# One block of state increments per unit, state products beside the chunk products, and a new table of steps

## The chip, the cores and the metric

One core of one Trainium2 chip runs the whole kernel. The metric is the device time of one execution in microseconds. Engines are named as the profile names them: PE is TensorE, ACT is ScalarE, DVE is VectorE, POOL is GpSimd, SP is SyncE; PE, ACT, DVE and POOL each run their own stream of instructions in program order, and SP mainly issues DMAs. PSUM is the memory into which TensorE writes its products.

## The reference, cut to what matters

```python
f = 1.0 / (1.0 + np.exp(-f_logit))
for t in range(S):                        # B, H, S, D = 4, 8, 768, 48
    state = f[:, :, t, :, None] * state + k_t v_t^T      # per batch and head, D x D
    y[:, :, t] = q_t @ state
x = y transposed to (B*S, H*D)            # 3072 x 384
h = x @ w_in                              # 384 x 2048
P = a0 + a1*h + a2*h**2 + a3*h**3
Q = 1 + |b0|*|h| + |b1|*h**2
out = (P / (Q + 1e-6)) @ w_out            # 2048 x 384
```

A gated linear recurrence over 768 time steps, then a feed-forward block whose activation is a rational function.

## The kernel before

**Units.** The time axis is cut into chunks of 128 steps, and two chunks of one batch element make a unit n = 4c + b (b the batch element, c = 0, 1, 2 the place in time). There are twelve units of 256 time steps. Each runs through the recurrence and then through the feed-forward block; the state of a batch element is handed from unit n to unit n + 4.

**The recurrence of a unit, by steps.** `ld` loads f, k, q and v. `ef` and `ls` (ACT) make the logarithms of the gates, `cs` (PE) sums them within a chunk, `A` (ACT, x = 0 or 1) takes the exponentials of the sums with either sign, `xa` (DVE) multiplies q and k by them, `T` (PE) and `Te` (DVE) transpose both. `sc` (PE) makes the scores within a chunk in two groups, `mk` (DVE) masks them, `vm` (POOL, or ACT in unit 0) copies pieces of v. `ya n j` (PE) does four things for chunk j: the products of q with the state at the beginning of the chunk (line 387, twelve products 128x32, left out where the state is zero), the increments k v of the chunk (line 410, sixteen products of 64 rows by 64 columns), the old state added to them through the identity (line 413), and, for j = 0, the decays summed over each chunk (line 417). `ae` (ACT) takes the exponential of the decays, `st n j` (DVE, line 446) multiplies and writes the state, in place: a batch element has one state buffer. So `ya n 1` waits for `st n 0`, and `st n j` may overwrite the state only after the products that read it. In the last third of the units (c = 2) chunk 1 needs no new state. `yb` (PE) adds the 64 products of the masked scores with v to the same y (64x32 each), and `ye` (ACT) writes y to SBUF as x.

**The feed-forward block.** `h` (PE) makes four of the sixteen blocks of 128 hidden units, in twelve products; `hy` (ACT) copies them. h squared comes from `sq` (DVE) or `sa` (ACT), |h| from `ab` (DVE). The denominator h^2 + |h| is summed either by `u` (PE, identity products into PSUM) and read by `ln` (ACT), or by `zd` (an adding DMA that POOL issues) or `zv` (DVE) and read by `lz` (ACT). `ex` (ACT) takes exp(-ln). `p1`, `p2`, `pm` (DVE), `ta` (an adding DMA) or `tv` (DVE), and `gm` (DVE) make the numerator and the quotient; `o` (PE) multiplies by w_out, `oe` copies, `so`, `s0`, `s1` store.

**What sets the order.** Everything. `ORDER` is a table of steps written out by hand or by a planner; the loop at the end of the kernel calls them one by one, and each engine gets its instructions in that order. Numbers after a step's name are the unit and blocks, `@i` is one of four PSUM slots of two banks each. A slot is given to the next step that names it once its last reader is done. `ya n 0 @i @j` takes a slot for y, which it holds until `ye`, and one for the state sums.

**The start.** `hv` writes two elements of w_in ahead of the load `wi 0 4`, so that this load waits for DVE to get there. a and b are loaded from ACT's queue (`ab_`), `fa` and `fb` (DVE) make the scaled coefficients, `rg` (ACT) loads two of them as registers, which `ye` and `ln` use. v of unit 0 comes as float32 into a buffer of its own, v32, and `vc` (ACT) casts it.

Of the kernel before, what the change touches and what calls it, by code (L numbers as in the profile page):

```python
# [19 lines left out]
ab_; cz 2; cb; ld 0 f 2 4; ld 0 f 0 2; ca; cz 3; ld 0 q 2 4; cz 1; ld 0 k 2 4; cz 0; cc; ld 0 k 0 2  # L20
ef 0 2 4; ls 0 2 4; ld 0 q 0 2; ef 0 0 2; fa; cs 0 2 4 @0; ls 0 0 2; ld 0 v; A 0 0 2 4; cs 0 0 2 @1
fb; A 0 1 2 4; xa 0 0 2 4; ld 1 f; rg; xa 0 1 2 4; A 0 0 0 2; T 0 2 4 @0; A 0 1 0 2; ld 1 k
Te 0 2 4; xa 0 1 0 2; sc 0 1 @0; ld 1 q; hv 0; xa 0 0 0 2; wi 4 8; mk 0 1; T 0 0 2 @1; vc 0
Te 0 0 2; vm 0 1 s; ya 0 0 @0 @2; vm 0 0 s; wi 0 4; sc 0 0 @1; ae 0; ef 1; ld 2 f; st 0 0; mk 0 0
ya 0 1; ls 1; ld 1 v; yb 0 2 4; st 0 1; yb 0 0 2; wi 8 16; cs 1 @1; ye 0; A 1 0; h 0 4 8 @0; A 1 1
hy 0 4 8; xa 1 1; ld 2 k; h 0 0 4 @0; xa 1 0; ld 2 q; hy 0 0 4; T 1 @1; ab 0 0 8; sq 0 0 8; ef 2
ld 3 f; Te 1; u 0 0 4 @0; ls 2; vm 1 1; ya 1 0 @2 @3; p1 0 0 8; vm 1 0; ln 0 0 4; ld 2 v; cs 2 @1
p2 0 0 8; ae 1; sc 1 0 @0; st 1 0; A 2 1; ld 3 k; mk 1 0; ya 1 1; A 2 0; xa 2 1; sc 1 1 @1
u 0 4 8 @0; st 1 1; mk 1 1; ln 0 4 8; ld 3 q; pm 0 0 8; ex 0 0 8; yb 1; h 0 12 16 @1; wo 8 12
xa 2 0; ye 1; wo 0 4; tv 0 0 8; ld 4 f; h 0 8 12 @0; ef 3; wo 4 8; gm 0 0 8; hy 0 12 16; wo 12 16  # L30
h 1 4 8 @2; hy 0 8 12; h 1 12 16 @1; ls 3; ld 4 k; sq 0 8 16; sa 1 4 8; vm 2 1; h 1 8 12 @0
p1 0 8 16; hy 1 12 16; ld 3 v; ab 0 8 16; hy 1 4 8; h 1 0 4 @3; vm 2 0; pm 0 8 16; hy 1 8 12
p2 0 8 16; u 0 12 16 @2; sa 1 0 4; ld 4 q; sq 1 8 16; u 0 8 12 @0; ln 0 12 16; T 2 @1; tv 0 8 16
ln 0 8 12; cs 3 @2; Te 2; hy 1 0 4; o 0 0 0 4 @0; o 0 1 0 4; A 3 1; ab 1 8 16; sc 2 0 @3; ab 1 0 8
A 3 0; u 1 12 16 @1; mk 2 0; ex 0 8 16; u 1 4 8 @2; ld 5 f; p1 1 0 16; u 1 0 4 @3; ln 1 4 8
o 0 1 4 8; gm 0 8 16; ln 1 12 16; o 0 0 4 8; p2 1 0 16; sc 2 1 @2; ln 1 0 4; o 0 1 8 12; u 1 8 12 @1
ef 4; mk 2 1; o 0 1 12 16; ex 1 0 8; pm 1 0 8; ya 2 0 @2 @3; ld 5 k; o 0 0 8 12; xa 3 1; ta 1 0 8
ae 2; ln 1 8 12; o 0 0 12 16; st 2 0; ls 4; xa 3 0; ya 2 1; ex 1 8 16; ld 5 q; pm 1 8 16; yb 2
T 3 @1; ld 4 v; st 2 1; ye 2; cs 4 @3; Te 3; ta 1 8 16; oe 0 0 2 s; h 2 12 16 @2; vm 3 1; A 4 1
ld 6 f; vm 3 0; A 4 0; sc 3 1 @1; xa 4 1; h 2 8 12 @0; hy 2 12 16; xa 4 0; so 0 0 2; ef 5  # L40
h 2 4 8 @3; mk 3 1; hy 2 8 12; sc 3 0 @2; gm 1 0 8; hy 2 4 8; h 2 0 4 @1; sa 2 4 8; mk 3 0; ld 6 k
o 1 0 0 4 @0; hy 2 0 4; o 1 0 4 8; sq 2 8 16; ld 5 v; sa 2 0 4; ya 3 0 @2 @3; ab 2 0 8; vm 4 1
o 1 1 0 4; ae 3; ab 2 8 16; ls 5; vm 4 0; o 1 1 4 8; zd 2 0 8; st 3 0; u 2 8 12 @1; p1 2 0 16
# [12 lines left out]
ya 5 1; mk 5 1; lz 4 0 8; so 2 0 2; cs 7 @0; zv 4 8 16; yb 5; u 3 8 12 @1; A 7 1; ld 8 v; st 5 1
ye 5; p1 4 0 16; T 6 @3; vm 7 0; ln 3 8 12; vm 7 1; h 5 4 8 @2; gm 3 0 8; A 7 0; ld 8 q; ex 3 8 16
h 5 12 16 @0; Te 6; p2 4 0 16; o 3 0 0 4 @3; ex 4 0 8; sc 6 1 @1; o 3 0 4 8; gm 3 8 16; o 3 1 0 4
ld 9 f; hy 5 12 16; xa 7 1; o 3 1 4 8; o 3 0 8 12; hy 5 4 8; mk 6 1; h 5 0 4 @0; sa 5 4 8; pm 4 0 8
ld 9 k; ef 8; h 5 8 12 @1; xa 7 0; ta 4 0 8; hy 5 0 4; o 3 0 12 16; pm 4 8 16; hy 5 8 12; sc 6 0 @2  # L60
o 3 1 8 12; sa 5 0 4; mk 6 0; ta 4 8 16; o 3 1 12 16; lz 4 8 16; ya 6 0 @0 @1; p1 5 0 16; ld 9 q
T 7 @2; ab 5 8 16; ae 6; oe 3 0 2 s; st 6 0; ex 4 8 16; sq 5 8 16; ya 6 1; so 3 0 2; yb 6; ab 5 0 8
u 5 8 12 @3; st 6 1; vm 8 0; ye 6; Te 7; zd 5 0 8; u 5 12 16 @1; ef 9; vm 8 1; ln 5 8 12; h 6 0 4 @0
pm 5 8 16; ld 9 v; ln 5 12 16; p2 5 0 16; h 6 12 16 @3; hy 6 0 4; ld 10 f; gm 4 0 8; ta 5 8 16
sc 7 0 @1; sa 6 0 4; h 6 8 12 @2; hy 6 12 16; mk 7 0; sc 7 1 @0; ls 8; o 4 0 0 4 @3; gm 4 8 16
hy 6 8 12; h 6 4 8 @1; mk 7 1; ld 10 k; ex 5 8 16; o 4 0 4 8; sq 6 8 16; ya 7 0 @0 @2; hy 6 4 8
pm 5 0 8; o 4 0 8 12; ae 7; sa 6 4 8; o 4 1 0 4; p1 6 0 16; ta 5 0 8; o 4 1 4 8; lz 5 0 8; ld 10 q
o 4 1 8 12; st 7 0; cs 8 @1; pm 6 0 8; ls 9; ya 7 1; pm 6 8 16; ex 5 0 8; yb 7; o 4 0 12 16; st 7 1
vm 9 0; ab 6 0 8; o 4 1 12 16; vm 9 1; ye 7; ld 10 v; ab 6 8 16; cs 9 @2; oe 4 0 2 s; gm 5 8 16
h 7 12 16 @0; zd 6 0 8; A 8 1; so 4 0 2; p2 6 0 16; A 8 0; h 7 4 8 @3; hy 7 12 16; xa 8 1; ta 6 8 16  # L70
h 7 8 12 @1; ef 10; xa 8 0; ta 6 0 8; ld 11 f; hy 7 4 8; h 7 0 4 @0; gm 5 0 8; hy 7 8 12; zv 6 8 16
T 8 @3; A 9 1; hy 7 0 4; o 5 0 0 4 @1; xa 9 1; o 5 1 0 4; lz 6 8 16; Te 8; o 5 0 4 8; ld 11 k
o 5 0 8 12; sq 7 0 8; A 9 0; sc 8 1 @3; sc 8 0 @0; ex 6 8 16; o 5 0 12 16; mk 8 1; o 5 1 4 8; xa 9 0
o 5 1 8 12; lz 6 0 8; ya 8 0 @3 @2; mk 8 0; ld 11 q; o 5 1 12 16; sq 7 8 16; ae 8; ex 6 0 8; T 9 @0
st 8 0; ab 7 8 16; ya 8 1; yb 8; ab 7 0 8; oe 5 0 2 s; u 7 8 12 @2; Te 9; vm 10 0; ye 8; zd 7 0 8
u 7 12 16 @1; ls 10; gm 6 8 16; vm 10 1; so 5 0 2; h 8 12 16 @0; ln 7 8 12; ld 11 v; gm 6 0 8
ln 7 12 16; sc 9 1 @2; cs 10 @3; p1 7 0 16; hy 8 12 16; h 8 8 12 @1; A 10 0; mk 9 1; ex 7 8 16
o 6 0 0 4 @0; p2 7 0 16; o 6 1 0 4; sc 9 0 @2; o 6 1 4 8; A 10 1; pm 7 0 8; o 6 1 8 12; hy 8 8 12
o 6 1 12 16; mk 9 0; ta 7 0 8; ef 11; ya 9 0 @1 @3; lz 7 0 8; pm 7 8 16; h 8 4 8 @2; xa 10 1
# [35 lines left out]
def kernel(  # L115
# [16 lines left out]
    P = 128  # L132
# [479 lines left out]
```

## Time and profile before

| | |
|---|---|
| median of three runs | 236.91 us (236.08 to 237.78) |
| span of the profiled execution | 231.9 us |
| granted TensorE clock, mean | 0.992 |
| `op` products with w_out (line 556) | 384, 69.7 us busy |
| `hp` products with w_in (line 455) | 576, 67.7 us |
| `u` identity products (line 489) | 88, 13.5 and 13.2 us |
| state increments `sv` (line 410) | 320, 9.2 us |
| state products of y (line 387, `qkT,state`) | 240, 7.2 us |
| `lq<-z` on ACT (line 513) | 13, mean 1952 ns |
| `lq<-u` on ACT (line 497) | 22, mean 1059 ns |
| `state` on DVE (line 446) | 20, mean 550 ns |
| adding DMAs `gall<-hy`, `z<-h` | 21 and 10, 512 KB each, 6.9 and 6.7 us from issue to landing |

A row of the profile's groups names the line, the engine, the operation and the tiles (out<-in), then the count, the busy time and the mean of one. Neighbouring instructions of one engine overlap a little in the records, so a sum of means is larger than an engine's busy time. The ends of matmuls are modelled. The slices cut the span into 40 equal parts, each digit a busy share in tenths. The chain of waits follows the work that ended last back to the start.

### The profile page before, as it was taken

Reading aid. Unit: us, or ns where it says so; the run is one execution under the profiler, and the core shown is the slowest. Engines: PE = TensorE matmul, PEld = TensorE weight load, DVE = VectorE, ACT = ScalarE, POOL = GpSimd, SP = SyncE. Lnnn points to the kernel's source line nnn. Section 1 sums busy time; section 2 is a strip of 40 time slices with the busy share of each in tenths; the row PEclk is TensorE's granted clock in tenths of the full one; section 3 lists DMA queues with packets and bytes.
Section 4 is the critical chain, followed back from the end, with each engine's and each line's share of the span. In section 5 each row is a group of like instructions: output and inputs, shape, how many; then the busy total and the mean of one; then the engine's idle time right before and its main releaser. Section 6 shows DMA issues by size and latency. Waiting matters only on the chain.

```text
span 231.9 us, 7110 instructions
## 1 busy us (share of the span) xinstructions
PE 211.8 (91%) x3120; PEld 146.2 (63%) x3120; DVE 205.4 (89%) x243; ACT 203.3 (88%) x216; POOL 67.7 (29%) x92
## 2 busy tenths in 40 slices
PE   0778679999999999999999999979999999999991
PEld 0455338745876768657767669556677687676550
DVE  6743778999899799999999999979999999899960
ACT  4455559999996999999999999889999999999970
POOL 7261620002405406135118058003231211340100
PEclk9999889999999999999999999999999999999999
DMA  6999999992999999999999968998970994999614
GB/s 146 229 232 204 235 203 203 244 248 72 158 237 251 145 174 231 144 173 183 246 203 215 236 126 154 210 211 164 133 148 16 181 200 82 187 197 204 123 52 119
DMA packets 61694, 41.28 MB, mean 178 GB/s; under 512 B 51424, under 2 KB 57312, under 8 KB 61664
## 3 DMA queue, kind: packets, MB, share of 16 engines
q0 software_dynamic: 19360, 21.57, 57.4%
q1 hardware_dynamic: 41856, 19.08, 35.7%
q8 instruction: 24, 0.39, 0.6%
q10 hardware_dynamic: 448, 0.20, 0.3%
q14 instruction: 6, 0.05, 0.1%
HBM read 25.17 MB, written 4.72 MB: 129 GB/s over the span
## 4 chain that ended last, share of the span: by engine, by line
PE 55%; DVE 21%; DMA 9%; ACT 9%; issue 4%; POOL 1%; POOLq 0%
PE op L556 18%; PE hp L455 15%; PE u L489 7%; DMA z<-h 4%; PE y L387 4%; DVE gall L536 4%; DMA v<-in_v_dram 3%; DVE scm L370 3%; ACT hy L469 3%; PE cs L316 2%; PE sv L410 2%; PE tp L341 2%; DVE gall L549 2%; DVE h L473 2%; DVE z L481 2%
## 5 line engine op out<-in xcount | busy, mean ns | idle before, releaser
L556 PE MATMUL op<-w_out_sb,gall 128*128 128x384 bf16 x384 | 69.7, 326 | 0.7 <-DVE osb L571 0.6
L455 PE MATMUL hp<-xT,w_in_sb 128*128 128x256 bf16 x576 | 67.7, 274 | 1.1 <-ACT hy L469 1.1
L455 PEld LDWEIGHTS <-w_in_sb 128*128 128x128 bf16 x576 | 55.9, 98 | 10.4 <-issue 1.6
L556 PEld LDWEIGHTS <-gall 128*128 128x128 bf16 x384 | 35.9, 98 | 23.8 <-issue 1.2
L469 ACT CAST hy<-hp 128x1024 bf16<-128x1024 f32 x48 | 48.8, 1040 | 2.1 <-PE hp L455 2.1
L521 ACT ACTIVATE qi<-lq 128x2048 bf16<-128x2048 f32 (+1 forms) x25 | 46.8, 1885 | 0.1
L540 POOL DMA_DIRECT2D gall<-hy x21 | 19.3, 969 | 66.7 <-ACT alast L442 24.4
L370 DVE TENSOR_TENSOR scm<-sc,mask 128x1024 bf16<-128x1024 f32 x24 | 29.0, 1216 | 2.6 <-PE sc L362 2.4
L549 DVE TENSOR_TENSOR gall<-gall,qi 128x2048 bf16<-128x2048 bf16 (+1 forms) x25 | 29.3, 1176 | 0.4 <-ACT qi L521 0.3
L536 DVE TENSOR_TENSOR gall<-gall,h 128x2048 bf16<-128x2048 bf16 (+1 forms) x25 | 29.2, 1174 | 0.0
L513 ACT ACTIVATE lq<-z 128x2048 f32<-128x2048 bf16 x13 | 25.4, 1952 | 1.8 <-DMA z<-h 1.8
L497 ACT ACTIVATE lq<-u 128x1024 f32<-128x1024 f32 x22 | 22.3, 1059 | 5.0 <-PE u L489 5.0
L381 POOL COPY vmp<-vn 128x128 bf16<-128x128 bf16 x22 | 16.4, 780 | 34.4 <-PE y L387 14.0
L325 ACT ACTIVATE A<-cs 128x768 f32<-128x768 f32 (+1 forms) x26 | 19.5, 788 | 1.7 <-PE cs L316 1.6
L506 POOL DMA_DIRECT2D z<-h x10 | 9.6, 956 | 37.0 <-ACT h L477 12.9
L473 DVE TENSOR_TENSOR h<-hy 128x2048 bf16<-128x2048 bf16 (+1 forms) x17 | 19.6, 1152 | 0.7 <-ACT hy L469 0.7
L481 DVE TENSOR_SCALAR z<-hy 128x2048 uint16<-128x2048 uint16 (+1 forms) x25 | 16.3, 669 | 2.6 <-ACT hy L469 2.6
L477 ACT ACTIVATE h<-hp 128x1024 bf16<-128x1024 f32 x16 | 17.1, 1070 | 0.0
L526 DVE TENSOR_SCALAR gall<-hy,a_sb 128x4096 bf16<-128x4096 bf16 (+2 forms) x15 | 17.1, 1138 | 0.0
L531 DVE TENSOR_SCALAR hy<-hy,a_sb 128x4096 bf16<-128x4096 bf16 (+2 forms) x15 | 16.9, 1125 | 0.1
L316 PE MATMUL cs<-lsp,Ui 128*128 128x384 bf16 (+1 forms) x39 | 11.6, 358 | 5.8 <-ACT lsp L306 5.8
L330 DVE TENSOR_TENSOR qkp<-kn,A 128x768 bf16<-128x768 f32 (+1 forms) x13 | 11.8, 909 | 4.5 <-ACT A L325 4.4
(70 smaller groups left out, 284.9 us busy)
## 6 DMA issues: line engine op xcount, KB each, us to landing
gall<-hy POOLq DMA_DIRECT2D x21, 512.0 KB, 6.9
z<-h POOLq DMA_DIRECT2D x10, 512.0 KB, 6.7
fn<-in_f_logit_dram SPq DMA_DIRECT2D x11, 384.0 KB, 7.8
kn<-in_k_dram SPq DMA_DIRECT2D x11, 384.0 KB, 9.2
qn<-in_q_dram SPq DMA_DIRECT2D x11, 384.0 KB, 8.2
out_dram<-osb SPq DMA_DIRECT2D x22, 192.0 KB, 4.0
vn<-in_v_dram POOLq DMA_DIRECT2D x11, 192.0 KB, 8.3
w_out_sb<-in_moe_w_out_dram POOLq DMA_DIRECT2D x4, 384.0 KB, 11.4
```

What stands on the lines that cost most here:

```text
L325: nc.scalar.activation(t, src, AF.Exp, scale=1.0 if x else -1.0)
L370: nc.vector.tensor_mul(t, s["sc", g].rearrange("s r a i t -> s (r a) (i t)"), mb)
L455: nc.tensor.matmul(t[:, m - m0, :].rearrange("f (j t) -> f j t", j=UB), w_in_sb[:, kk, m * P:(m + 1) * P], s["x"][:, :, kk, :], start=(kk ...
L469: nc.scalar.copy(fl(big(s, "hy", "hy", 3), m0, m1), fl(s["hp", m0], 0, m1 - m0))
L473: nc.vector.tensor_mul(fl(big(s, "h2", "h2", 2), m0, m1), fl(s["hy"], m0, m1), fl(s["hy"], m0, m1))
L481: nc.vector.tensor_scalar(fl(big(s, "z", "z", 2), m0, m1).bitcast(U16), fl(s["hy"], m0, m1).bitcast(U16), 0x7FFF, None, op0=ALU.bitwise_and)
L497: nc.scalar.activation(fl(s["lq", g], m0 - 8 * g, m1 - 8 * g), fl(s["u", m0], 0, m1 - m0), AF.Ln, scale=rsig2, bias=1.0 + 1e-6)
L513: nc.scalar.activation(fl(s["lq", g], m0 - 8 * g, m1 - 8 * g), fl(s["z"], m0, m1), AF.Ln, scale=rsig2, bias=1.0 + 1e-6)
L521: nc.scalar.activation(fl(s["qi", g], m0 - 8 * g, m1 - 8 * g), fl(s["lq", g], m0 - 8 * g, m1 - 8 * g), AF.Exp, scale=-1.0)
L536: nc.vector.tensor_mul(fl(s["g"], m0, m1), fl(s["g"], m0, m1), fl(s["h2"], m0, m1))
L549: nc.vector.tensor_mul(fl(s["g"], m0, m1), fl(s["g"], m0, m1), fl(s["qi", g], m0 - 8 * g, m1 - 8 * g))
L556: nc.tensor.matmul(s["op"][:, j, 0:DM], s["g"][:, m, C * j:C * j + C], w_out_sb[:, m, :], start=(m == 0), stop=(m == KF - 1))
```

## The change

The state of a batch element gets three buffers that are used in turn, so `st n j` writes a new one instead of the one it read. That frees the products of y with the state from their place: they move from `ya` to the head of `yb`, next to the chunk products, and y takes its slot only there. `ya` is split into `sv`, which makes the increments of both chunks in one run, the chunks (that is, the two row halves) alternating, and `id n j`, which adds the old state and, for j = 0, the decays. The three buffers need room, which v32 gives up: it uses one of the output buffers. a and b are loaded from SP's queue. The table of steps is new from end to end; the `u`, `ln`, `lz`, `zv`, `sa` and `sq` steps in it differ in number. Its purpose is that the state chain no longer holds up the y products, that TensorE changes its shape of product less often, and that slots are held for less time.

```diff
 ORDER = """
...
-ab_; cz 2; cb; ld 0 f 2 4; ld 0 f 0 2; ca; cz 3; ld 0 q 2 4; cz 1; ld 0 k 2 4; cz 0; cc; ld 0 k 0 2
-ef 0 2 4; ls 0 2 4; ld 0 q 0 2; ef 0 0 2; fa; cs 0 2 4 @0; ls 0 0 2; ld 0 v; A 0 0 2 4; cs 0 0 2 @1
-fb; A 0 1 2 4; xa 0 0 2 4; ld 1 f; rg; xa 0 1 2 4; A 0 0 0 2; T 0 2 4 @0; A 0 1 0 2; ld 1 k
-Te 0 2 4; xa 0 1 0 2; sc 0 1 @0; ld 1 q; hv 0; xa 0 0 0 2; wi 4 8; mk 0 1; T 0 0 2 @1; vc 0
-Te 0 0 2; vm 0 1 s; ya 0 0 @0 @2; vm 0 0 s; wi 0 4; sc 0 0 @1; ae 0; ef 1; ld 2 f; st 0 0; mk 0 0
-ya 0 1; ls 1; ld 1 v; yb 0 2 4; st 0 1; yb 0 0 2; wi 8 16; cs 1 @1; ye 0; A 1 0; h 0 4 8 @0; A 1 1
-hy 0 4 8; xa 1 1; ld 2 k; h 0 0 4 @0; xa 1 0; ld 2 q; hy 0 0 4; T 1 @1; ab 0 0 8; sq 0 0 8; ef 2
-ld 3 f; Te 1; u 0 0 4 @0; ls 2; vm 1 1; ya 1 0 @2 @3; p1 0 0 8; vm 1 0; ln 0 0 4; ld 2 v; cs 2 @1
-p2 0 0 8; ae 1; sc 1 0 @0; st 1 0; A 2 1; ld 3 k; mk 1 0; ya 1 1; A 2 0; xa 2 1; sc 1 1 @1
-u 0 4 8 @0; st 1 1; mk 1 1; ln 0 4 8; ld 3 q; pm 0 0 8; ex 0 0 8; yb 1; h 0 12 16 @1; wo 8 12
-xa 2 0; ye 1; wo 0 4; tv 0 0 8; ld 4 f; h 0 8 12 @0; ef 3; wo 4 8; gm 0 0 8; hy 0 12 16; wo 12 16
-h 1 4 8 @2; hy 0 8 12; h 1 12 16 @1; ls 3; ld 4 k; sq 0 8 16; sa 1 4 8; vm 2 1; h 1 8 12 @0
...
+cz 2; ca; ld 0 f 2 4; ld 0 f 0 2; cz 1; ld 0 q 2 4; cz 0; cb; cz 3; ld 0 k 2 4; cc; ef 0 2 4
+ld 0 k 0 2; ls 0 2 4; ld 0 q 0 2; ef 0 0 2; cs 0 2 4 @0; ls 0 0 2; ld 0 v; A 0 1 2 4; cs 0 0 2 @1
+A 0 0 2 4; ab_; xa 0 0 2 4; A 0 0 0 2; A 0 1 0 2; xa 0 1 2 4; ld 1 f; hv 0; T 0 2 4 @1; wi 0 4
+xa 0 1 0 2; xa 0 0 0 2; Te 0 2 4; ld 1 k; T 0 0 2 @0; ld 1 q; wi 4 8; sc 0 1 @1; Te 0 0 2; vc 0
+mk 0 1; sc 0 0 @0; vm 0 0 s; sv 0 @2; vm 0 1 s; mk 0 0; ld 1 v; id 0 0; fa; wi 8 16; ae 0; st 0 0
+rg; fb; id 0 1; yb 0 0 4 @0; st 0 1; ef 1; ld 2 f; ls 1; ye 0; cs 1 @2; h 0 0 4 @0; A 1 0; A 1 1
+xa 1 1; ld 2 k; h 0 4 8 @2; hy 0 0 4; hy 0 4 8; xa 1 0; ld 2 q; sv 1 @0; vm 1 0; sq 0 0 8; id 1 0
+ld 2 v; T 1 @2; ae 1; vm 1 1; ab 0 0 8; st 1 0; u 0 4 8 @1; Te 1; ef 2; ld 3 f; id 1 1; u 0 0 4 @3
+ln 0 4 8; st 1 1; sc 1 1 @2; p1 0 0 8; ls 2; sc 1 0 @0; mk 1 0; ln 0 0 4; cs 2 @1; mk 1 1; ex 0 0 8
+ld 3 k; p2 0 0 8; yb 1 0 4 @2; A 2 1; pm 0 0 8; h 0 8 12 @0; wo 4 8; A 2 0; xa 2 1; wo 12 16; ye 1
+h 0 12 16 @1; ld 3 q; wo 0 4; tv 0 0 8; hy 0 8 12; wo 8 12; h 1 4 8 @2; xa 2 0; hy 0 12 16; ld 4 f
...
 """
...
-    states = [consts.tile([P, HP, 2 * D], BF16, name=f"state{b}") for b in range(B)]
+    states = [[consts.tile([P, HP, 2 * D], BF16, name=f"state{b}_{i}") for i in range(3)] for b in range(B)]
...
-            units[n] = dict(c=c, b=b, qk=qkp[n % 2], ls=lsp[n % 2], vm=vmp[n % 2], st=states[b])
+            units[n] = dict(c=c, b=b, qk=qkp[n % 2], ls=lsp[n % 2], vm=vmp[n % 2],
+                            st=[states[b][(UB * c + j) % 3] for j in range(UB + 1)], begun=set())
...
-            s[what] = consts.tile([P, H, 2, D], F32, name="v32")
+            s[what] = _at(ms.tile([P, UB, DM], F32, name="osb"), [[2 * D, H], [D, 2], [1, D]])
...
     def load_ab():
-        nc.scalar.dma_start(out=b_sb, in_=bass.AP(tensor=moe_b.tensor, offset=moe_b.offset,
+        nc.sync.dma_start(out=b_sb, in_=bass.AP(tensor=moe_b.tensor, offset=moe_b.offset,
...
-    def ya(n, j, *args):
...
+    def sv(n, sl):
+
+        s = unit(n)
+        t = slot(sl, [P, UB, 512], F32, "sv")
...
+        for a in range(HP):
+            for i in range(2):
+                for j in range(UB if s["c"] < NCC - 1 else 1):
                     for par in range(2):
...
+    def add(n, j):
+
+        s = unit(n)
+        nc.tensor.matmul(s["sv"][:, j], ident, s["st"][j], start=False, stop=True, skip_group_check=True)
         if j == 0:
...
+    def yb(n, a0, a1, sl=None):
+
+        s = unit(n)
+        if sl is not None:
+            s["y"] = slot(sl, [P, UB, 512], F32, "y")
+        for j in range(UB):
+            if s["c"] + j > 0:
+                for kk in range(KD):
+                    for a in range(a0, a1):
+                        ymm(s, j, a, kk, s["st"][j][:, a, 32 * kk:32 * kk + 32], s["T"][:, 0, :, a, R * j:R * j + R])
...
-        nc.vector.tensor_mul(s["st"], s["sv"][:, j], _at(s["ae"], [[1, HP], [0, 2 * D]], HP * j))
+        nc.vector.tensor_mul(s["st"][j + 1], s["sv"][:, j], _at(s["ae"], [[1, HP], [0, 2 * D]], HP * j))
```

The last two lines of both tables are the same. Counted over the whole table:

| step | before | after |
|---|---|---|
| `u`, `ln` | 22 each | 28 each |
| `lz` | 13 | 10 |
| `zv` | 3 | 0 |
| `sa` | 16 | 14 |
| `sq` of 8 blocks | 15 | 16 |
| `zd`, `ta` | 10, 21 | 10, 21 |

## The prediction

> **What bounds the kernel now.** I read the page's busy shares and its 40 slices first, then the table of waits, then the start in order of time, then TensorE alone in the steady part.
>
> ```profile
> span 231.9 us, 7110 instructions
> ...
> PE 211.8 (91%) x3120; PEld 146.2 (63%) x3120; DVE 205.4 (89%) x243; ACT 203.3 (88%) x216; POOL 67.7 (29%) x92
> ...
> PE   0778679999999999999999999979999999999991
> ...
> DVE  6743778999899799999999999979999999899960
> ACT  4455559999996999999999999889999999999970
> ```
>
> Three engines are full together from slice 7 (about 40 us) to slice 37. No single one is "the bound" there; what can be won is the filling before 40 us, the small holes after it, and the load of whichever engine is fullest. The table of waits (engine, what it waited for: us in total, times, longest) says how small the holes are:
>
> ```profile
> PE cs L316 <- ACT lsp L306: 5.8, 2, 5.6
> PE y L387 <- DVE state L446: 2.1, 4, 1.4
> PE u L489 <- DVE h L473: 2.1, 1, 2.1
> PE sv L410 <- ACT vn L206: 1.5, 1, 1.5
> PE hp L455 <- ACT hy L469: 1.1, 1, 1.1
> PE y L387 <- DVE scm L370: 1.0, 1, 1.0
> ```
>
> Only the y wait on the state (1.8 of its 2.1 us fall after 60 us, by the same table cut at 60 to 220 us) is spread over the run; the others are in the filling. The start in order of time (start, us, engine, line) shows what the filling hangs on:
>
> ```profile
> 12.00 0.83 ACT L206 CAST vn<-v 128x768 bf16<-128x768 f32 x1 [3.72 <-DMA v<-in_v_dram]
> ...
> 14.38 0.56 DVE L446 TENSOR_TENSOR state<-sv,alast 128x384 bf16<-128x384 f32 x1 [2.23 <-ACT alast L442]
> ...
> 19.07 2.02 PE L455 MATMUL hp<-xT,w_in_sb 128*128 128x256 bf16 x12
> ...
> 22.18 1.47 PE L455 MATMUL hp<-xT,w_in_sb 128*128 128x256 bf16 x12 [1.10 <-ACT hy L469]
> ```
>
> v lands at 12.0, the first FFN products start at 19.07, and the second group waits until ACT has emptied the first, because both use slot 0. Later `yb 1` ends at 35.41 and the group `h 1 4 8` at 39.4 (third of a back-to-back run that starts at 35.41, 1.31 us each).
>
> TensorE alone, one unit in the steady part:
>
> ```profile
> 82.73 0.35 PE L387 MATMUL y<-qkT,state 128*32 128x128 bf16 x12
> 83.01 0.43 PE L410 MATMUL sv<-vn,qkp 64*64 64x48 bf16 x16
> 83.38 0.34 PE L413 MATMUL sv<-state,ident 128*128 128x384 bf16 x1
> ...
> 86.05 0.35 PE L387 MATMUL y<-qkT,state 128*32 128x128 bf16 x12
> 86.33 0.43 PE L410 MATMUL sv<-vn,qkp 64*64 64x48 bf16 x16
> 86.69 0.34 PE L413 MATMUL sv<-state,ident 128*128 128x384 bf16 x1
> ```
>
> Twelve state products take 0.28 us of the engine (82.73 to 83.01), sixteen increments 0.36 to 0.37. One product lasts 0.19 us (the row of L410: 186 ns), so the sixteen starts span 0.24 us, 16 ns apart, and some 0.13 us passes from the last start to the next kind of product.
>
> [...] the y pieces, which use both row halves, start 8 ns apart (64 within 86.96 to 87.47), the increments, which use one row half at a time, 16 ns[...]. [...] `yb` took 1.39 us at the start and 0.67 later, and the granted clock is 0.85 from 20 to 30 us. [...] up to 12.2 us q1 (f, q, k, v) had 69.5% of the engines' time and q0, on which half of w_in is loaded, 21.1%. [...]
>
> **The change on each engine.** TensorE price of a step, from the chain of waits where it runs back to back: h 1.31 us, four o 0.65, u 0.86, T 0.89, cs 0.65, sc 0.35, state y 0.28, sv 0.36, identity 0.2, alast 0.2, yb 0.67. Before: 48 h 62.9, 96 o 62.4, 22 u 18.9, 12 T 10.7, 12 cs 7.8, 24 sc 8.4, 20 state y 5.6, 20 sv 7.2, 20 identity 4.0, 12 alast 2.4, 12 yb 8.0: 198.3 us.
>
> (a) Increments of both chunks at once, state y ahead of the pieces. Products stay the same in number (320 and 240). Mode changes fall: a unit with c = 0 has seven before and five after, c = 1 eight and five, c = 2 six and five, so 4 x (2 + 3 + 1) = 24 fewer at 0.12 to 0.13 us: 2.9 us. Alternating row halves can bring 32 increments from 16 ns apart to 8: 0 to 0.26 us in each of 8 units, 0 to 2.0. Bounds: 1.7 [...] to 4.9; I take 3.5.
> (b) The new table also shifts work. u goes from 22 to 28 steps: 6 x 0.86 = 5.2 us more on TensorE. ACT: ln 22 to 28, lz 13 to 10, sa 16 to 14; spaced at 0.93, 1.85 and 0.93 us (a row's mean less some 0.1 us by which neighbours overlap): +5.6 - 5.6 - 1.9 = -1.9. DVE: three zv away, one sq more, at 1.13: -2.3. No DMA-added sum is added or lost (10 zd, 21 ta).
> (c) Three states in turn and y taken late: state y of a chunk no longer has to stand between the state's reading and its overwriting. In the new table state 0 of units 4 to 8 is written 7 to 16 us of TensorE work ahead of its `yb`, against 0 to 2 us before. That takes the 1.8 us of waits away. The wait it adds is `id n 1` on `st n 0`; queued behind it are h, o and u, but 0 to 1.2 us of other products stand between, as before between st and `ya n 1`. I cost it at nothing more.
> (d) a and b are loaded behind v on SP, and coef_a runs on DVE between mk and the first st. coef_a took 1.6 us in the page's start (4.24 to 5.84); `rg` on ACT waits for it. Seven us of slack are lost, so it may lie on the path: walked below.
> (e) v32 uses an output buffer: no instruction, and its reader ends long before the first output. Zero.
>
> **The filling, walked with the durations of before.** w_in is held until `hv`, now at about 8.4 us, where before half of it ran from 3 us on against f, q, k, v. q0's 21.1% of 12.2 us is 2.6 us, so v lands at about 10. DVE then sets the pace: both Te end at 11.3, two mk at 1.21 at 13.7, coef_a at 15.3, st at 15.9. `yb 0` [...] ends at 17.9, ye 18.7: the first h starts at 18.8, little earlier than 19.07. But its second group has slot 2 of its own: h ends at 22.1, hy at 23.2 (24.7 before). sq and ab end at 25.1, st, Te and st at 27.4, p1 at 28.2, two mk at 30.6, `yb 1` at 31.5 (35.41 before). Meanwhile ACT: ln, ls, ln, ex to 30.7, two A to 32.2, ye 33.1. `h 1 4 8` ends at 35.4 instead of 39.4: 4.0 us ahead. Bounds: 1.5, if w_in or v of unit 1, now behind all of `wi 0 4` and `wi 4 8` on POOL's queue, land late (v of unit 1 came at 22.2 before); 5, if the clock stays up.
>
> **From there to the end.** Before, steps up to `h 1 4 8` are 17.9 us of TensorE work; 198.3 - 17.9 = 180.4 remain, done between 39.4 and 227.7 (last product, 4.2 us ahead of the span's end): 95.8% filled. After, 200.0 in all, 17.5 done, 182.5 remain. (c) takes 1.8 of the 7.9 us of holes away: 96.7%. 182.5 / 0.967 = 188.7, so the last product is at 35.4 + 188.7 = 224.1, 3.6 us earlier. The last two lines of the table are the same, so is the tail. ACT and DVE allow more: 1.9 and 2.3 us of work less and the same head start, about 6 us. TensorE is the fullest and decides. 236.9 - 3.6 = 233.3.
>
> **Rivals.** *TensorE eats it*: the head start is 2.5 and the filling stays 95.8%: 36.9 + 190.5 = 227.4, 0.3 earlier, 236.6 us. For: u's 5.2 us go to the engine with the highest busy share. Against: ACT and DVE get lighter, and the slots are used more evenly (31 allocations of slot 3 before, 37 after). *All three get the whole*: head start 5, holes halved to 2.3% since zd and ta in the middle get 13 to 18 us of other work before their reader instead of 8 to 13, and a single z<-h delay cost 10.1 us of the chain at 141 us: 34.4 + 182.5 / 0.977 = 221.2, 230.4 us. *Slower*: the head start is 1.5 for want of w_in or coef_a, (a) saves only 1.7 (184.3 remain), and new holes make 95.3%; the new zd of units 8 and 10 have only 5 to 6 us before `lz`, and z<-h took 4.5 to 7.9: 37.9 + 193.4 = 231.3, 3.6 later, 240.5 us.
>
> **How the numbers follow.** Forecast 0.52, TensorE eats it 0.23, the whole 0.12, slower 0.13. The range goes from 230, just past the third case, to 238, past the second; the slower case is left out. Faster by over 1% (under 234.5): most of the forecast and the whole, 0.60. Slower by over 1%: 0.13. Between: 0.27.
>
> **What would show it.** (a) right if 32 increments take 0.4 to 0.6 us up to the next kind of product, wrong at 0.7. (b) the two u rows x56 instead of x44, the lq<-z row x10 instead of x13, no z<-z,h row. (c) no `PE y <- DVE state` wait after 60 us. (d) v cast at about 10, first st near 15.3. Filling: second sq or ab before 25.5, `h 1 4 8` ending near 35.4. If the page shows that head start and a last product later than 226, the filling of TensorE after it was the wrong step; if the head start is missing, the walk was.

## The result, and the profile after

| | before | after |
|---|---|---|
| median, first comparison | 236.62 us (236.08 to 237.78, four runs) | 229.28 us (227.44 to 231.46, four runs) |
| ratio after / before | | 0.9657, 95% interval 0.9571 to 0.9744 |
| second comparison (e1) | 237.12 us | 228.35 us, ratio 0.9654 (0.9582 to 0.9727) |

The change takes 3.4% away, some 8 us; 233.3 us had been forecast, with a range down to 230. The first profiled execution of the changed kernel (231.46 us) was the slowest of its four, so the lines below come from the one taken in e1 (228.99 us), which is the same kernel. Times are medians of all executions of a kernel in one comparison, but ratios leave out those that lie more than 1.5% above the fastest of the same kernel, so the two can differ a little.

The page of the changed kernel (e1): span, busy times, slices.

```profile
span 227.3 us, 7126 instructions
...
PE 208.3 (92%) x3127; PEld 147.1 (65%) x3144; DVE 202.6 (89%) x241; ACT 201.6 (89%) x217; POOL 74.6 (33%) x92
...
PE   1758879999999999999999999999999999999991
...
DVE  4773999899999999999879999999999998989950
ACT  5546579999999999999999999999997899999950
```

The three engines are still full together, now from slice 6 (about 34 us) on. ACT's share between 60 and 180 us rose from 115.5 to 118.1 us of 120, TensorE's from 118.1 to 119.0, DVE's from 115.4 to 116.3: all three are packed more densely, none by much.

The table of waits of the changed kernel (e1), TensorE's rows (what it waited for: us in total, times, longest):

```profile
PE cs L319 <- ACT lsp L309: 5.2, 3, 4.8
PE sv L412 <- DVE state L453: 2.6, 2, 2.4
PE sv L405 <- DMA vn<-in_v_dram: 1.5, 1, 1.5
PE y L390 <- DVE scm L373: 1.4, 1, 1.4
```

The waits of y for the state and of u for h are gone. What is left lies in the filling; in the same table cut at 60 to 220 us no row of TensorE is over 0.4 us.

The start in order of time (e1; start, us, engine, line):

```profile
9.14 0.83 ACT L209 CAST vn<-osb 128x768 bf16<-128x768 f32 x1 [1.69 <-DMA osb<-in_v_dram]
...
14.04 0.55 DVE L453 TENSOR_TENSOR state<-sv,alast 128x384 bf16<-128x384 f32 x1
...
17.82 3.90 PE L462 MATMUL hp<-xT,w_in_sb 128*128 128x256 bf16 x24
...
23.27 0.55 PE L405 MATMUL sv<-vn,qkp 64*64 64x48 bf16 x32 [1.55 <-DMA vn<-in_v_dram]
...
31.38 5.25 PE L462 MATMUL hp<-xT,w_in_sb 128*128 128x256 bf16 x36
```

v is cast at 9.14 instead of 12.00, and the first two h groups run back to back from 17.82. `h 1 4 8`, the last of the three groups that start at 31.38, starts at 35.15 and, with the step's 1.31 us, ends at 36.5 instead of 39.3 (39.4 in the forecast). The wait of 1.55 us on v of unit 1 is new.

The three groups took 5.25 us here. In e13, which is the changed kernel once more, they start at 31.37 and take 4.09 us. The granted clock differs, first e1, then e13:

```profile
PEclk9999969999999999999999999999999999999997
```

```profile
PEclk9999999999999999999999999999999999999998
```

From 20 to 40 us its mean is 0.91 in e1 and 1.00 in e13; the 6 in e1 is the slice from 28.4 to 34.1 us. The first of the three groups took 2.46 us up to the start of the second in e1, 1.31 in e13.

TensorE in the steady part (e1), a unit's increments and a unit's y:

```profile
60.24 0.42 PE L405 MATMUL sv<-vn,qkp 64*64 64x48 bf16 x32
60.59 0.34 PE L412 MATMUL sv<-state,ident 128*128 128x384 bf16 x1
...
82.88 0.52 PE L390 MATMUL y<-qkT,state 128*32 128x128 bf16 x24
83.33 0.25 PE L390 MATMUL y<-scm,vn 64*32 64x128 bf16 x8
```

32 increments take 0.35 us up to the next kind of product, as long as 16 took before; 24 state products take 0.45 us where two runs of 12 took 0.28 each.

The groups (e1) show the shift from the vector sums to TensorE:

```profile
L504 ACT ACTIVATE lq<-u 128x1024 f32<-128x1024 f32 x28 | 29.9, 1084 | 0.9 <-PE u L496 0.9
L520 ACT ACTIVATE lq<-z 128x2048 f32<-128x2048 bf16 x10 | 19.7, 1974 | 1.2 <-DMA z<-h 1.2
L496 PE MATMUL u<-z,ident 128*128 128x512 bf16 x56 | 16.6, 379 | 0.8
```

56 u products a row (44 before), 10 `lq<-z` (13 before), and no row in which DVE adds h into z.

### The profile page after: what moved, and what is told of

Read it like the earlier page. It is cut to its first block, busy times and chain, and to the rows that moved or that the text cites. A ratio compares the mean times of both kernels' runs of the same rounds, so it can differ in the third digit from the quotient of the medians.

```text
span 229.8 us, 7143 instructions
## 1 busy us (share of the span) xinstructions
PE 210.4 (92%) x3144; PEld 147.0 (64%) x3144; DVE 203.4 (89%) x241; ACT 202.1 (88%) x217; POOL 73.4 (32%) x92
## 4 chain that ended last, share of the span: by engine, by line
PE 35%; DVE 21%; DMA 20%; ACT 17%; issue 5%; SPq 1%; POOLq 0%; ACTq 0%
PE op L563 13%; PE hp L462 10%; DMA fn<-in_f_logit_dram 7%; ACT hy L476 5%; DMA z<-h 5%; DVE scm L373 5%; PE u L496 4%; ACT qi L528 3%; DMA vn<-in_v_dram 3%; DVE gall L543 2%; DMA w_in_sb<-in_moe_w_in_dram 2%; DVE gall L556 2%; DVE h L480 2%; PE y L390 2%; ACT lq L504 2%
## 5 line engine op out<-in xcount | busy, mean ns | idle before, releaser
L462 PE MATMUL hp<-xT,w_in_sb 128*128 128x256 bf16 x576 | 70.8, 279 | 1.5 <-ACT osb L578 0.8
L462 PEld LDWEIGHTS <-w_in_sb 128*128 128x128 bf16 x576 | 57.0, 100 | 13.0 <-issue 2.8
L547 POOL DMA_DIRECT2D gall<-hy x21 | 20.3, 1002 | 58.0 <-DVE hy L538 24.4
L384 POOL COPY vmp<-vn 128x128 bf16<-128x128 bf16 x22 | 21.2, 981 | 27.8 <-DMA vn<-in_v_dram 13.9
L504 ACT ACTIVATE lq<-u 128x1024 f32<-128x1024 f32 x28 | 28.9, 1051 | 0.0
L480 DVE TENSOR_TENSOR h<-hy 128x2048 bf16<-128x2048 bf16 (+1 forms) x18 | 21.1, 1172 | 4.4 <-ACT hy L476 4.4
L520 ACT ACTIVATE lq<-z 128x2048 f32<-128x2048 bf16 x10 | 19.4, 1943 | 1.6 <-DMA z<-h 1.6
L496 PEld LDWEIGHTS <-ident 128*128 128x128 bf16 x112 | 10.7, 98 | 10.4 <-issue 1.6
L496 PE MATMUL u<-h,ident 128*128 128x512 bf16 x56 | 16.7, 379 | 0.6 <-ACT hy L476 0.4
L496 PE MATMUL u<-z,ident 128*128 128x512 bf16 x56 | 16.6, 379 | 0.1
```

The lines of the kernel that those rows point to most:

```text
L384: nc.gpsimd.tensor_copy(dst, src)
L462: nc.tensor.matmul(t[:, m - m0, :].rearrange("f (j t) -> f j t", j=UB), w_in_sb[:, kk, m * P:(m + 1) * P], s["x"][:, :, kk, :], start=(kk ...
L480: nc.vector.tensor_mul(fl(big(s, "h2", "h2", 2), m0, m1), fl(s["hy"], m0, m1), fl(s["hy"], m0, m1))
L496: nc.tensor.matmul(t[:, m - m0:m - m0 + 2, :].rearrange("p m t -> p (m t)"), ident, fl(src, m, m + 2), start=(x == 0), stop=(x == 1))
L504: nc.scalar.activation(fl(s["lq", g], m0 - 8 * g, m1 - 8 * g), fl(s["u", m0], 0, m1 - m0), AF.Ln, scale=rsig2, bias=1.0 + 1e-6)
L547: nc.gpsimd.dma_start(out=fl(s["g"], m0, m1), in_=fl(s["hy"], m0, m1), accum_op=ALU.add)
```

## The experiments

Each ratio is to the kernel before in the same comparison. Milestones are in us of the profiled execution; "rest" is the time from the end of `h 1 4 8` (its start and 1.31 us) to the end of the last product. "y and sv" is what the increments, identity and decay products and all y products of units 2 to 11 (1208 products) take on TensorE, each group at its median time up to the next kind of product; for the changed kernel it shifts by up to 0.8 us if groups are also told apart by what follows them.

| profile | y and sv | `h 1 4 8` ends | last product | rest |
|---|---|---|---|---|
| before (233.56 us) | 22.9 | 39.3 | 227.7 | 188.4 |
| before again, e5 (235.91) | 22.9 | 41.3 | 230.0 | 188.8 |
| old table, joined increments, e12 | 20.9 | 39.3 | 226.3 | 186.9 |
| old table, whole structure, e4 | 19.9 | 39.1 | 224.4 | 185.3 |
| after, first comparison (231.46, the slowest of four) | | 37.3 | 225.6 | 188.3 |
| after, e1 (228.99) | 19.3 | 36.5 | 223.1 | 186.7 |
| after, e13 (227.72) | 19.6 | 35.3 | 221.8 | 186.5 |

**e1, the changed kernel again.** No edit; its numbers stand above.

> The changed kernel once more, for a profile that compares with the one of before. If the head start was the mis-sized step, h 1 4 8 ends at 34 us or earlier and the last product follows some 188 us later; if the filling of TensorE after it was, h 1 4 8 ends near 35.4 and the last product follows after 185 us or less. Time 228 to 230 us.

**e5, the kernel before again.** No edit. It tells how far one profiled execution may stand from the median.

> The kernel before, unchanged, for a second profile: the first came from an execution of 233.6 us, while its median is 237. If the filling is what makes the usual execution longer, this profile has a span of some 235 us and yb 1 and h 1 4 8 come 2 to 4 us later than 34.7 and 39.4. If the steady part varies, they come at the same time and the 3 us are lost after 60 us.

235.4 us beside 236.16, ratio 0.998 (0.9951 to 1.0008): no difference. But this profile (235.91 us, close to the median) is 2.35 us longer than the one the forecast was built on (233.56 us). The start tells where: v is cast at 13.71 instead of 12.00, the first h starts at 20.77 instead of 19.07, and the lag remains: the last product comes 2.3 us later. Nor is the first profile an ordinary one: 233.56 us is below all 58 executions of before in this comparison (233.7 to 239.7), and v was cast at 12.00 us in it, but at 12.88, 13.45 and 13.71 in e12, e4 and e5, which start with the same loads. The profile of before that I priced was a lucky one. Why these loads came earlier in it no run shows.

**e4, the structure alone, under the old table.**

```diff
-ya n 0 @y @sv   ... ya n 1 ... yb n
+sv n @sv; id n 0 ... id n 1 ... yb n 0 4 @y
```

The three states and the joined runs are those of the changed kernel; the order of everything else, u, zv and the loads are those of before.

> The new functions (three states, increments of both chunks in one run, state products at the head of the chunk products) under the old table of steps: each first ya becomes sv and id 0, each second id 1, yb takes y's slot; a and b loaded from ACT as before. If the structure is what saves (24 changes of mode, the waits on the state), 3 to 5 us under the kernel before: 232 to 233.5. If the new table saves, by its filling and its spacing, 0 to 1.5 us under the kernel before: 235 to 236.6.

230.93 us, ratio 0.9774 (0.9705 to 0.9842): 5.3 us less. About two thirds of the whole effect come without the new table.

**e12, the increments joined, but the state products of y at their old places.**

```diff
-ya n 0 @y @sv   ... ya n 1
+ys n 0 @y; sv n @sv; id n 0 ... ys n 1; id n 1
```

> The old table with increments of both chunks in one run and three states, but the products of y with the state at their old places in ya. Against the new functions under the old table (some 5.3 us under the kernel before) this splits the gain. By the step prices read from the traces, the joined increments save 0.3 to 0.4 us in each of 8 units, some 3 us, and the moved state products the rest, with their waits: so 2 to 3.5 us under the kernel before. If the move of y is what saves, 0 to 1.5 us; if the increments are, 4.5 to 5.5 us.

232.31 us, ratio 0.9875 (0.9828 to 0.9921): 2.9 us less. So joining the increments is about half of e4's gain and moving y the other half, though the two stem from different comparisons and their intervals touch. In the table above, TensorE's price falls by 2.0 (e12) and 3.0 us (e4) against e5, the rest by 1.9 and 3.5 us: in these profiles what TensorE was spared came back after the start, about one to one. Both profiles are also some 2 us ahead of e5's at the end of `h 1 4 8`, but level with the first profile of before, so how much of that is the edit's is not shown.

**e2, the chunks one after the other inside the joined run.**

```diff
-        for a in range(HP):
-            for i in range(2):
-                for j in range(UB if s["c"] < NCC - 1 else 1):
+        for j in range(UB if s["c"] < NCC - 1 else 1):
+            for a in range(HP):
+                for i in range(2):
```

> The changed kernel with the loops of the increments turned: all sixteen products of chunk 0, then all of chunk 1, in the same step. If alternating row halves overlaps the products, sv of 32 takes 0.6 us or more up to the next kind of product instead of 0.45 or less, in 8 units, and the time rises by at most 2 us (some 230.5). If row halves do not matter, no change: 229.3.

229.85 us, ratio 0.9682 (0.9601 to 0.9763), beside 0.9654 for the changed kernel of the same comparison: not told apart as a time. As a price it is plain. TensorE of this kernel at the same place:

```profile
60.39 0.57 PE L405 MATMUL sv<-vn,qkp 64*64 64x48 bf16 x32
60.89 0.34 PE L412 MATMUL sv<-state,ident 128*128 128x384 bf16 x1
```

0.50 us instead of 0.35, and instead of 0.36 twice when the chunks were apart. The products and the place are the same in both kernels, so the 0.15 us are what alternating the row halves brings here.

**e3, w_in loaded as before, under the new table.** `wi 4 8` goes first and unheld, `hv` and `wi 0 4` stand later.

```diff
-... xa 0 1 2 4; ld 1 f; hv 0; T 0 2 4 @1; wi 0 4
-xa 0 1 0 2; xa 0 0 0 2; Te 0 2 4; ld 1 k; T 0 0 2 @0; ld 1 q; wi 4 8; ...
+... xa 0 1 2 4; ld 1 f; T 0 2 4 @1; wi 4 8
+xa 0 1 0 2; hv 0; xa 0 0 0 2; Te 0 2 4; ld 1 k; T 0 0 2 @0; ld 1 q; wi 0 4; ...
```

> The changed kernel with the order of the first w_in loads as before: w_in blocks 4 to 8 are not held, blocks 0 to 4 are held until DVE has made half of the second k. If v was late because of w_in, v of unit 0 is cast at about 12 us instead of 9.8, but DVE's chain (masks, coefficients, state) goes on to about 15, so h starts at about 19 and the time rises by 0 to 0.7 us. If the load order is what makes the head start, h 1 4 8 ends 2 us or more later and the time is 231.5 or more.

235.69 us, ratio 0.9893 (0.9786 to 0.9999): by the ratios (0.9654 for the changed kernel of the same comparison) some 5.7 us of the gain are lost by the order of two loads. The start in order of time of this kernel:

```profile
25.80 0.96 DVE L333 TENSOR_TENSOR qkp<-qn,A 128x768 bf16<-128x768 f32 x1 [4.44 <-DMA qn<-in_q_dram]
...
26.82 1.39 PE L344 MATMUL tp<-ident,qkp 128*128 128x128 bf16 x16 [3.64 <-DVE qkp L333]
```

q of unit 1 is used at 25.80 where the changed kernel has it at 20.48, and TensorE's transposes wait behind it; f of unit 2 is late by 3.3 us for the same reason. v of unit 0, for whose sake I thought w_in was held, is not what is lost: x of unit 0 is written at 17.4 us here and at 16.6 there. What holding w_in buys is the loads of unit 1 and 2. In this profile `h 1 4 8` ends 2.9 us later than in e1 and the rest is 3.0 us longer.

**e6, the same edit in the other direction: before, with w_in held.**

```diff
-... xa 0 1 2 4; A 0 0 0 2; ...  hv 0; xa 0 0 0 2; wi 4 8; ...  wi 0 4; ...  h 0 4 8 @0 ... h 0 0 4 @0
+... xa 0 1 2 4; hv 0; A 0 0 0 2; ...  xa 0 0 0 2; wi 0 4; ...  wi 4 8; ...  h 0 0 4 @0 ... h 0 4 8 @0
```

> The kernel before with only the first w_in loads as in the changed one: all of w_in waits until DVE has made the first half of q and k, blocks 0 to 4 come first and are used first. If the load order by itself makes the head start, the time falls by 3 us or more, to 234 or less, and yb 1 comes 2 us earlier or more. If it helps only where the table can use the earlier loads, 236 to 237.5.

234.01 us, ratio 0.9924 (0.9896 to 0.9952): 1.8 us less. Under the old table the same edit is worth about a third of what undoing it costs under the new one.

**e16, v of unit 1 ahead of `wi 4 8`,** on top of e8 (the next experiment below), to take away the new wait of `sv 1`.

```diff
-ld 1 q; wi 4 8; ...  mk 0 0; ld 1 v; id 0 0
+ld 1 q; ld 1 v; wi 4 8; ...  mk 0 0; id 0 0
```

> The changed kernel with the coefficients early and with v of unit 1 loaded ahead of w_in blocks 4 to 8. The coefficients alone brought the first state forward but not yb 1, since the increments of unit 1 waited for v until 23 us. If v is what holds them, they start at about 21 us and the time falls by 1 to 2 us against the changed kernel. If w_in blocks 4 to 8 now come late, or k and q of unit 1 are the next to hold, no change.

233.51 us, ratio 0.9887 (0.986 to 0.9915), beside 0.9686 for the changed kernel of the same comparison (e13): 4.7 us worse. The second h group now started at 24.2 us for want of its quarter of w_in (21.1 in e8) and `h 1 4 8` started at 38.6 (34.7). The 1.5 us wait was the cheaper end of a trade.

**e8, the coefficients as early as before,** a and b loaded first of all on ACT's queue and `fa`, `fb` ahead of `xa 0 0 2 4`.

```diff
-A 0 0 2 4; ab_; xa 0 0 2 4; ...  id 0 0; fa; wi 8 16; ae 0; st 0 0
+A 0 0 2 4; fa; fb; xa 0 0 2 4; ...  id 0 0; wi 8 16; ae 0; st 0 0
```

> The changed kernel with a and b loaded from ACT's queue at the start and the coefficients made ahead of the first qk product on DVE, as before. If the 1.5 us of coefficients between the masks and the first state lie on the path of the filling, the first state comes at about 13.2 us instead of 14.7, the first h 1 to 1.5 us earlier, and the time falls by about 1 us. If v of unit 1 or its k and q hold up the next stage anyway, no change: 228.5.

229.15 us, ratio 0.9768 (0.9693 to 0.9844), where e1 has 0.9654 and e13 0.9686: no gain. The wait of TensorE for the first states shrank from 2.6 to 1.2 us, but `sv 1` then waited for v of unit 1 all the same (1.7 us), and `h 1 4 8` ended at 36.0, 0.7 us after that of e13, whose granted clock was 1.00 from 20 to 40 us like this one's. So step (d)'s 1.6 us lay on a path that a transfer closes a little later.

**e7, part of u turned back into zv,** for blocks 8 to 16 of units 4, 6 and 8.

```diff
-u 4 8 12 @0; ... ln 4 8 12; u 4 12 16 @1; ... ln 4 12 16
+zv 4 8 16; ... lz 4 8 16
```

> The changed kernel with three pairs of u and ln turned back into zv and lz (second halves of units 4, 6 and 8, the ones that the table before gives to zv): 5.2 us of work less on TensorE, 3.4 us more on DVE, the same on ACT. If TensorE sets the end, as the prediction has it, the time falls by 2 us or more, to 227 or less. If DVE and ACT set it, it rises by 1 to 3.4 us, to 229.5 to 232.

232.49 us, ratio 0.9857 (0.9827 to 0.9887): some 4 us slower than the changed kernel (0.9654 and 0.9686 in other comparisons; none ran in this one), though TensorE has 5.2 us less to do. Three zv of 1.13 us are added on DVE, without a new plan around them. Its profiled execution (235.65 us) lay above its median: `h 1 4 8`, ahead of every edited step, ended at 40.1 us, 3.6 us later than in e1. The rest is 189.7 us, 3.0 us longer than in e1, and from 60 to 180 us TensorE was busy 112.9 of the 120 us, where it had 119.0.

**e9, e10, e11: one engine made lighter at a time.** e9 passes only |h| through the identity (u leaves h squared out); e10 leaves `p2` of whole units out; e11 leaves `ef` out and lets `ls` take the exponential.

```diff
-        for x, src in ((0, s["h2"]), (1, s["z"])):
+        for x, src in ((1, s["z"]),):
...
     def p2(n, m0, m1):
+        if m1 - m0 == 16:
+            return
...
     def ef(n, a0=0, a1=HP):
+        return
...
-   s["f"][:, hh], AF.Ln, bias=1.0)
+   s["f"][:, hh], AF.Exp, scale=-1.0)
```

The first edit is e9's, the second e10's, the last two are e11's. Kernels that leave work out compute something else; only their time is of use.

> The changed kernel with half of each u left out (only |h| goes through the identity, h squared is not added): some 12 us of TensorE work less, nothing else changed. If TensorE sets the end, as the prediction has it, the time falls by 6 us or more, to 222 or less. If DVE or ACT sets it, it falls by 0 to 2 us, to 226.5 to 228.5.

> The changed kernel without p2 over whole units (a1*h + a0 is not formed, the numerator adds h itself): ten operations at 1.25 us less on DVE, 12.5 us. If DVE sets the end, the time falls by 6 us or more, to 222 or less; if it is one of two full engines, by 1 to 4 us; if TensorE sets it alone, by less than 1 us.

> The changed kernel without ef (the gate's logarithm is replaced by its exponential, made in one step): 11 operations of 0.78 us and two halves less on ACT, 9.5 us. If ACT sets the end, the time falls by 5 us or more, to 223.5 or less; if it is one of two full engines, by 1 to 3 us; if TensorE sets it alone, by less than 1 us, save for 0.8 us in the filling.

| | taken off (estimate) | time | ratio |
|---|---|---|---|
| changed kernel (e1, e13) | | 228.35, 228.35 | 0.9654, 0.9686 |
| e9 | TensorE, 12 us | 230.58 | 0.9733 (0.9671 to 0.9794) |
| e10 | DVE, 12.5 us | 228.38 | 0.9707 (0.9664 to 0.9751) |
| e11 | ACT, 9.5 us | 228.29 | 0.9714 (0.9668 to 0.9761) |

The estimates are step prices and means; in the profiles the busy time fell by 7, 11 and 7 us against e1. Not one of the three moves the time by more than the comparisons can tell. Their rests are 187.4, 185.6 and 186.1 us, where the changed kernel has 186.7 and 186.5. Where the chain of waits runs instead is told by the page. Its shares by engine, for e9 and then for e10:

```profile
ACT 41%; DVE 23%; DMA 16%; PE 11%; issue 8%; POOLq 0%; ACTq 0%; DVEq 0%
```

```profile
PE 49%; ACT 34%; DMA 8%; DVE 4%; issue 3%; ACTq 0%
```

With a lighter TensorE the chain runs over ACT and DVE; with a lighter DVE, over TensorE and ACT. The shares are a rough guide: in three profiles of the unchanged new kernel (first comparison, e1, e13) TensorE has 35 to 53%, ACT 14 to 20% and DVE 8 to 24%.

**e13, e14, e15: several at once.** e13 is the changed kernel again, for the comparison; e14 joins the edits of e10 and e11; e15 joins all three.

> The changed kernel again, as the measure for the other three of this call: 228 to 229 us.

> The changed kernel without p2 over whole units and without ef, both at once: 12.5 us less on DVE and 9.5 us less on ACT, TensorE unchanged. Each alone changed nothing. If the three engines are equally full, and the fullest of them sets the end, TensorE still holds some 198 us of work, so the time falls by 1 to 4 us only. If DVE and ACT are what counts and TensorE has room, it falls by 6 us or more. If the end is set by waits that no engine's work makes up, no change.

> The changed kernel with half of each u, without p2 over whole units and without ef: 12, 12.5 and 9.5 us less on TensorE, DVE and ACT. If the three engines are equally full and the fullest sets the end, the time falls by 7 us or more, to 221 or less. If waits and transfers set it, it falls by less than 3 us.

e13 228.35 us, 0.9686 (0.9622 to 0.9749); e14 227.1 us, 0.9618 (0.9564 to 0.9673); e15 225.75 us, 0.957 (0.9518 to 0.9621). With the work of every full engine cut by 9.5 to 12.5 us, only 2.6 us come out. Cutting the trace at the same work shows where. From the end of `ye 2` to the end of `ye 11`, in us:

| | time | TensorE busy | ACT busy | DVE busy |
|---|---|---|---|---|
| changed, e13 (50.3 to 194.8) | 144.5 | 143.6 | 141.9 | 139.4 |
| DVE and ACT lighter, e14 (51.7 to 194.3) | 142.6 | 142.4 | 137.6 | 128.7 |
| all three lighter, e15 (51.4 to 190.8) | 139.4 | 136.7 | 136.5 | 128.3 |

In this stretch 5.1 us come out, about as much as ACT's busy time falls (5.4), and in each row some engine is busy 98% or more. So here the gain fits engines that are level with one another and full. More than half of it is lost again outside the stretch: `ye 2` ends 1.1 us later than in e13, though no later than in e1 (51.5), and from the end of `ye 11` to the end of the kernel e15 takes 33.3 us, e13 31.2.

**e17, e18: the transfers that add.** The chain of e15 still had 20% in DMA, so both leave `zd` and `ta` out, e17 from the changed kernel and e18 from e15.

```diff
     def zd(n, m0, m1):
+        return
...
     def ta(n, m0, m1):
+        return
```

> The changed kernel without the 31 sums that a DMA adds: zd (h squared onto the absolute value, read by lz) and ta (second linear part onto the first, read by gm); lz then reads the absolute value alone and gm the first part alone, every other instruction stays. If the wait of lz and gm for these transfers (some 6 us each from issue to landing) is what sets the pace after 40 us: 219 to 224 us, ratio to before 0.93 to 0.95. If the pace is set by the three engines' hand-overs in the order of the table, with the transfers hidden behind other work: 227 to 229, ratio 0.96 to 0.97, as the changed kernel.

> The kernel of e15 (u through the identity only for the absolute value, no p2 of whole units, no ef: about 12 us less on each of TensorE, VectorE and ScalarE) and in addition without the 31 added sums zd and ta. If the transfers are what kept e15 at 225.7 us although each engine had 10 us less to do: 213 to 219, ratio 0.90 to 0.93. If the order of the hand-overs did: 223 to 226, ratio 0.95 to 0.957. If it falls under 219 while the changed kernel without the sums stays at 227 to 229, engines and transfers share the bound, each hiding the other.

e17: 230.25 us, 0.9705 (0.9553 to 0.9858); e18: 223.98 us, 0.9499 (0.9403 to 0.9595). The changed kernel gains nothing without the transfers, and the lighter one some 1.8 us more, with intervals that overlap and four executions each: they are not what sets the end as far as these runs tell. The chain of e17:

```profile
PE 80%; DMA 9%; ACT 6%; DVE 3%; issue 1%
```

and of e18:

```profile
PE 40%; ACT 31%; DVE 14%; DMA 9%; issue 3%; SPq 1%; ACTq 0%
```

Without the transfers the chain of the changed kernel is TensorE's work almost throughout, and the time stays. In e18 TensorE stands idle 4.3 us between 42 and 200 us, in e13 1.2 and in e1 1.9: a part of what it was spared it spends waiting there, and the longest waits are for slots that ACT still reads. All TensorE waits over 0.4 us of e18 between 60 and 210 us:

```profile
PE op L566 <- ACT lq L503: 1.1, 1, 1.1
PE hp L461 <- ACT lq L503: 0.7, 1, 0.7
PE y L389 <- ACT osb L581: 0.5, 1, 0.5
```

and ACT, with 4% less busy time over the whole, is busy 117 of 120 us from 60 to 180. From the end of `ye 2` to the end of `ye 11` e18 takes 139.3 us, as e15 does. Why the other stretches do not get shorter with it is open: no run changed the order of the table for the lighter kernels.

## Why the prediction was wrong

**The base: wrong, and the largest error.** The gain was worked out on a profile of 233.56 us (last product 227.7) and then taken from a median of 236.9. The forecast's own last product, 224.1, was nearly met (223.1 in e1, 221.8 in e13). Taken from the execution it belongs to, the forecast would have been 233.56 - 3.6 = 230.0. e5 shows where the two differ: in an ordinary execution of before the loads of the start come 1.7 us later and the end 2.3 us later. The durations of the walk gave the changed kernel's start in absolute terms, and the "before" it was compared with was a good one. This step, "236.9 - 3.6 = 233.3", accounts for 3.3 of the 4.0 us of error. Between the ordinary executions e5 and e1 (e13) the head start is 4.8 us (6.0), where 4.0 was forecast.

**Filling TensorE after the start: mis-sized by 2 us.** "(c) takes 1.8 of the 7.9 us of holes away: 96.7%". The work of that stretch is 180.4 + 5.2 for u, less 3.3 to 3.6 for (a), so 182.0 to 182.3, in 186.7 us (e1) or 186.5 (e13): 97.5 to 97.7%. Of 7.9 us of holes some 3.5 went. The rest of 188.7 forecast was 186.7 and 186.5; in the slowest execution of the first comparison it was 188.3. The rival *All three get the whole* had this term right (97.7%).

**"TensorE is the fullest and decides": fits the old table, wrong under the new.** In e12 and e4 the rest falls by nearly what TensorE's price falls. In the changed kernel 12 us off TensorE do nothing (e9), and giving it 5.2 us less at the cost of DVE and ACT makes some 4 us more (e7). So the 5.2 us of (b) were not a burden. The new table's rest is only 1.3 us longer than e4's with about 5 us more TensorE work, and it starts 2.6 to 3.8 us ahead. I read the lower load of ACT and DVE as what closes the holes; e7 supports that for the u steps, but its table was not planned anew, so part of its 4 us may be disorder. Not shown.

**(a): right.** 32 increments take 0.35 us, a little under the 0.4 to 0.6 expected. Over units 2 to 11 the price falls from 22.9 us to 19.3 (e1) and 19.6 (e13), by 3.3 to 3.6; 3.5 was taken for all units, of which 3.1 lay after the start. The 0.12 to 0.13 us for each change of mode, that is of the kind of product, were an estimate from the gap after the last start in the trace of before. What e2 shows is 0.22 us for one run of 32 instead of two of 16 (0.50 instead of 0.36 twice) and 0.15 us for the alternation; how much of the 0.22 is the change itself is not shown.

**(b) and (c): right in what they show.** u rows x56, `lq<-z` x10, no vector sum; no y wait on the state after 60 us, where 1.8 us had been.

**The walk through the filling: right to the end of `yb 1`, then 1.1 us late in e1, at a lowered granted clock.** v was cast at 9.14 (about 10 forecast), the first state started at 14.04 (15.3), the second h squared and |h| ended at 24.0 and 24.7 (25.1), and the three h groups after `yb 1` started at 31.38 (31.5). `h 1 4 8` ended at 36.5 (35.4) in e1, where the first of the three groups took 2.46 us and the granted clock was 0.91 from 20 to 40 us, and at 35.3 in e13, where they were 1.31 us and 1.00. That it met 31.5 is in part luck: the wait of 1.55 us on v of unit 1 was named only as a bound, and the first state came 1.3 us earlier than the walk had it. Against the same profile of before the changed kernel is 2.9 (e1) and 4.0 us (e13) ahead. What I did not see is that holding w_in mainly serves k, q and f of units 1 and 2 (e3). The shares of the two DMA queues in the forecast (69.5 and 21.1%) show that both moved data in the same 12 us; that v gains the 2.6 us of q0 was an estimate. With w_in loaded as before (e3) v is cast at 11.58 us, with w_in held (e1) at 9.14. And the 1.39 us of `yb 0` in the profile of before (16.42 to 17.81) are not the granted clock's, which was 1.00 from 16 to 18 us there; why later ones take 0.67 no run shows.

**(d): the path it was priced on was real** (TensorE waited 2.6 us for the first states), but removing it gained nothing (e8).

For each execution the terms add up, as they must; what they show is the sizes: 233.3 - 3.3 for the base, - 2.0 for the filling after the start, + 1.1 for the h group at the lowered clock (2.46 instead of 1.31 us), is 229.1 (e1: 228.99); 233.3 - 3.3 - 2.2 - 0.1 is 227.7 (e13: 227.72).

## What to carry to other kernels

Take a gain worked out on a profile from the time of that very execution, after comparing it with the median; if they differ, find the difference in the trace first, for it may lie in the stage being priced. Where several engines are over 88% busy, do not let the fullest one decide by its busy share: take some 5% off one engine at a time and see which one moves the time. Here none did. Compare profiles stage by stage, between the same two steps: a difference that stands before the first edited step is not the edit's. In a filling, price each load that a change delays by the readers of all the loads that now overtake it, not only by its own.

## What the runs showed of the hardware that was not expected

32 products of 64x64 in alternating row halves take as long (0.35 us) as 16 in one half (0.36 us); one half after the other they take 0.50 us. Executions of the same kernel before in one comparison ran from 233.7 to 239.7 us (58 runs), and the two profiled ones already differ by 1.7 us at the first cast of v, before most of the work has begun. The granted clock goes with the time: in the 37 of the 58 with a mean of 0.99 or more the median is 235.6 us, in the other 21 237.3. From 20 to 40 us the mean granted clock is 0.91 in the profiles of before, the first comparison, e1, e3, e5, e15 and e18, 0.83 in e6 and e7, and 1.00 in e4, e8 and e13. In e1 one group of twelve products took 2.46 us there, in e13 1.31.
